# Fixed tensors for the probability buffers, and another sharing of the values products among a pair's five units

## The chip, the cores and the metric

The kernel runs on one core of one Trainium2 chip. The metric is the device time of one execution in microseconds (us), lower is better. Before the change three runs took 487.65, 487.83 and 488.74 us, so the median is 487.83 us.

## The reference

What is computed is an attention with a learned position bias, followed by a gated feed-forward stage with a convolution of three taps along the sequence. There are 4 batches, 8 heads, 576 positions and 64 columns per head; the feed-forward stage goes from 512 to 1024 and back to 512 columns.

```python
scores = scale * np.matmul(q, k.transpose(0, 1, 3, 2))
x = (psi_rel / psi_i)[..., None]
bias = np.maximum(x @ w1 + b1, 0.0) @ w2
scores = scores + bias.transpose(2, 0, 1)[None]
attn = np.exp(scores - scores.max(-1, keepdims=True))
attn = attn / (attn.sum(-1, keepdims=True) + 1e-09)
x = (attn @ v).transpose(0, 2, 1, 3).reshape(B, S, H * D)
h = np.maximum(x @ w_in, 0.0)
conv_out[i] = conv_w[0] * h[i - 1] + conv_w[1] * h[i] + conv_w[2] * h[i + 1]
out = (h / (1 + np.exp(-conv_out))) @ w_out
```

## The kernel before, in words

The program has three stages. In the first, some 65 us long, the bias table is computed on PE, DVE and ACT and stored to DRAM, and the first units of attention are slipped in. The second is attention, up to about 290 us. The third is the feed-forward stage, up to the end.

**Pairs and units.** Attention runs over 16 *pairs*: two heads of one batch (`seq`, index `n` from 0 to 15). The 576 query rows of a pair are cut into five *units* `t`: unit 0 holds the first 64 rows of both heads, units 1 to 4 hold 128 rows of each of the two heads. `flat` lists the units in order, pair after pair from `n = 1` on, with two units of pair 0 slipped in near the start; the list has 77 entries and `u` counts them. The main loop `for u, (n, t) in enumerate(flat)` works on three units at a time:

- `scores` (L364): products of the queries and keys of unit `u + 2` on PE, for one head after the other, each into one of the two PSUM buffers `s` (pool `psS`);
- `reduce` (L375): DVE adds the bias, scales, writes the result into a buffer `sp` in SBUF and keeps the row minimum in `nm`, for each head;
- `expo` (L389): ACT takes the exponential of unit `u + 1` in place in `sp`;
- `turned_sp` (L341 to L344): gives the buffer its second name `sr`, of the type that PE transposes (float32r). `sp` and `sr` are tiles of one pool under one tag, and ACT writes 128x2 elements of the new tile, behind the row (L343, the *tiny write*);
- `side_transposes` and `transposes` (L423, L435): PE turns the probabilities of unit `u`, 18 small products for a unit of two heads and 10 for unit 0. The last two of the 18 go into the free end of the PSUM buffer `s` of the scores just made (`side`); the other 16 go into two of three PSUM buffers `tp` (pool `psT`). Unit 2 of a pair also turns the row sums of the pair before (L427);
- copies (L92 on ACT, L95 on DVE): ACT copies the first `tp` buffer, DVE the `side` end and then the second `tp` buffer, into `ptx` (units 0 to 2) or `pty` (units 3 and 4);
- `part` (L472, from `pv_parts`): a *part* is two products of the turned probabilities with the values; five parts make the output of `ptx` (320 columns) and five that of `pty` (256 columns). The five of `ptx` are put into the queue `fill` when unit 2 is turned, those of `pty` when unit 4 is. The last part is followed by ACT's copy of the output from PSUM (L92, `x<-o`).

PE takes up to `pv_share[ui]` parts from `fill` after the transposes of unit `ui`. Before, the table is (2, 2, 1, 3, 2): units 3 and 4 do the five parts of `ptx`, units 0, 1 and 2 of the next pair those of `pty`. From `u = 7` (unit 0 of pair 2) on this table sets the order; before that the parts are taken as they come, and `u = 5` and `u = 6` (units 3 and 4 of pair 1) have none behind their transposes. Every product of scores and values stands as two records in the profile, every transpose as one.

Beside this, every second unit carries a job (`split_w_steps`) that prepares weights for the feed-forward stage: a shift on DVE (L101), a step on ACT (L103), a second shift on DVE in the next unit (L107), and two operations on GpSimd. The jobs start in every other unit; since a pair has five units, they fall on units 1 and 3 of the pairs with odd `n` (3 to 13) and on units 0, 2 and 4 of those with even `n`.

The order on each engine is the order of the program text. What holds an operation back is a buffer: the second head's scores need the `s` buffer that held the last unit's second head, so they wait for DVE's `reduce` and for DVE's copy of the `side` end; the second transpose of a unit needs the `tp` buffer that ACT copied in the unit before.

In the feed-forward stage `gt` and `hr` hold the last 64 rows of each batch; before, they are tiles of the pools `wo` and `hr`.

The lines that the change touches are L311 (the pool `sp`), L324, L330 to L344 (`new_sp`, `turned_sp`), L681 (`pv_share`), L783 (`gt`) and L859 (`hr`).

Of the kernel before, what the change touches and what calls it, by code (L numbers as in the profile page):

```python
# [9 lines left out]
F32 = mybir.dt.float32  # L10
F32R = mybir.dt.float32r
I32 = mybir.dt.int32
AF = mybir.ActivationFunctionType
# [6 lines left out]
def attention_ffn_kernel(  # L20
# [11 lines left out]
    nc = tc.nc  # L32
    B, S, DM = out.shape
# [5 lines left out]
    P = 128  # L39
    TL = S % P  # L40
# [4 lines left out]
    FC = DFF // P  # L45
# [13 lines left out]
    def pool(stack, name, bufs, **kw):  # L59
        return stack.enter_context(tc.tile_pool(name=name, bufs=bufs, reuse_waits="tile", **kw))  # L60

    const = pool(ctx, "const", 1)
    bias_c = const
    dram = ctx.enter_context(tc.tile_pool(name="dram", bufs=1, space=DRAM))
# [50 lines left out]
    def narrow(tp, raw, tags=("u", "w")):  # L115
        w, u = narrow_tiles(tp, raw, tags)
        for _ in narrow_steps(w, u, raw):
            pass
        return w.bitcast(F32)
# [19 lines left out]
    with tc.manual_schedule():  # L139
        att = ExitStack()  # L140
# [64 lines left out]
        pars = bias_c.tile([P, par.shape[1]], F32, name="pars")  # L205
# [102 lines left out]
            nc.sync.dma_start(dst[:, :, 0:nr + nf], st[:, :, 0:nr + nf])  # L308


        sp_p = pool(att, "sp", 1)  # L311
        ptx_p = pool(att, "ptx", 1)
        pty_p = pool(att, "pty", 1)
        sm_p = pool(att, "sm", 4)
# [6 lines left out]

        xb = {0: x0}
        spt, ptt, nms, exps = {}, {}, {}, {}
        SPB = 3  # L324
        DATA = mybir.DependencyInfo(mybir.DependencyClass.Sync, mybir.DependencyReason.DATA)

        def new_sp(n, t):  # L330
            tag = f"sp{len(nms) % SPB}"
            tile = sp_p.tile([P, 2 * S + 2], F32, name="sp", tag=tag)
            if t:
                spt[n, t] = (tile[:, 0:2 * S].rearrange("p (h j) -> p h j", h=2), tag)
            else:
                if n == 0:
                    nc.vector.memset(tile[:, 0:TL], 0.0)
                    nc.vector.memset(tile[:, TL + S:P + S], 0.0)
                spt[n, t] = (tile[:, TL:TL + S].rearrange("p (h j) -> p h j", h=1), tag)

        def turned_sp(n, t):  # L341
            tile = sp_p.tile([P, 2 * S + 2], F32R, name="sr", tag=spt[n, t][1])
            nc.scalar.activation(tile[:, 2 * S:], pars[:, 0:2], AF.Copy)  # L343
            spt[n, t] = (tile, None)  # L344


        def scores(n, t, h):
# [194 lines left out]
        xr, hr = [], []  # L542
# [129 lines left out]
        for h in heads(flat[0][1]):  # L672
            expo(*flat[0], h)
        turned_sp(*flat[0])
        while fill:
            fill.popleft()()
# [1 line left out]
        psT = pool(ctx, "psT", 3, space=PSUM)  # L678
        psO = pool(ctx, "psO", 1, space=PSUM)
        psum.update(s=psS, tp=psT, o=psO)  # L680
        pv_share = (2, 2, 1, 3, 2)  # L681
        hs_ff = {}
        raw_w = {}
        job_steps = iter(())
# [3 lines left out]
        for u, (n, t) in enumerate(flat):  # L688
            p, b = seq[n]
# [14 lines left out]
            if u + 1 < NU:  # L704
                for h in heads(flat[u + 1][1]):
                    expo(*flat[u + 1], h)
                turned_sp(*flat[u + 1])
# [11 lines left out]
            if u + 2 >= NU:  # L719
                f = u + 2 - NU  # L720
# [55 lines left out]
        wo_p = pool(ff, "wo", 1)  # L776
        g_p[0] = pool(ff, "g", FC + 4)
        e2_p = pool(ff, "e2", 2)
        hr_p = pool(ff, "hr", 1)
        o_p = pool(ff, "oo", 3)  # L780

        wo += [wo_p.tile([P, 2, DM], F32R, name=f"wo{f}") for f in range(FE, FC)]
        gt = [wo_p.tile([P, 2, P], F32R, name=f"gt{f}") for f in range(FC)]  # L783

        def tap(b, f, h):
            cv = (e2_p if f % 4 > 1 else e_p).tile([P, S], F32, name="cv")
# [69 lines left out]
                    if 0 <= j - k < FC:  # L856
                        stage(b * FC + j - k, k)

        hr += [hr_p.tile([P, B - 1, TL], F32, name=f"hr{f}") for f in range(FC)]  # L859
        ws = [narrow(tp, raw_o[0][:, k], ("cv", "cv")) for k, tp in enumerate((e_p, e2_p))]  # L860
        xr.append(xa_p.tile([P, KC, 2, B, TL], F32R, name="xr", tag="x"))
        x_rest(0)
# [7 lines left out]
        for b in range(B):  # L870
# [25 lines left out]
            for c in range(KC):  # L896
# [5 lines left out]
                lambda f, gi, t=t: gs[b, f][:, gi, t * P:(t + 1) * P] for t in range(NT)  # L902
# [98 lines left out]
```

## Time and profile before

| what | value |
|---|---|
| median of three runs | 487.83 us |
| profiled execution, first to last instruction | 485.4 us |
| granted TensorE clock in the profiled execution | 1.000 |
| PE busy, weight loads (PEld) busy | 469.5 us (97%), 332.0 us (68%) |
| DVE busy | 361.1 us (74%) |
| ACT busy | 316.6 us (65%) |
| GpSimd (POOL) busy | 147.2 us (30%) |
| share of PE in the chain of work that ended last | 85% |

The profiled execution is known by its span alone, 485.4 us; it lies 2.4 us below the median of the runs, which is the time around the first and the last instruction. Busy times are those of the engines between these two instructions. A PE that the profile shows as busy may still have gaps, since the ends of products are modelled; the weight loads (PEld) show more plainly when PE's queue moved on, and their starts are used below as the clock of PE's queue. One row of a timeline has the start, the time it covers, the engine, the line, the operation, what is written and read with shapes, the number of records, and in brackets the idle time before it and what released it.

### The profile page before, as it was taken

The page shows a single profiled execution, that of the slowest core. Times are in us where ns is not written, and L with a number is a line of the kernel's source. Part 1 is how long each engine was busy: PE and PEld are TensorE (multiplying, and loading weights), DVE is VectorE, ACT ScalarE, POOL GpSimd, SP SyncE. Part 2 cuts the span into 40 slices and gives each one's busy share as a digit, 9 for nine tenths or more (in the row PEclk, how much of TensorE's full clock was granted, in tenths as well). Part 3 has the DMA queues.
Part 4 walks back from the last instruction along what each step waited for, and adds up shares of the span by engine and source line. Part 5 has one row for each costly group of instructions (what it writes and reads, how often), then busy time and mean ns, then how long its engine had stood idle before and what let it go on. Part 6 is the DMA issues. An engine that isn't in the chain of part 4 may idle for free.

```text
span 485.4 us, 10556 instructions
## 1 busy us (share of the span) xinstructions
PE 469.5 (97%) x3914; PEld 332.0 (68%) x3914; DVE 361.1 (74%) x873; ACT 316.6 (65%) x791; POOL 147.2 (30%) x221
## 2 busy tenths in 40 slices
PE   5978899999999999999999999999999999999996
PEld 2333366666666666666666668988888888888886
DVE  6999976788898889988897821694489238936971
ACT  6999886798888889888888832772254125424530
POOL 1000001355445726556446728006000600060000
PEclk9999999999999999999999999999999999999999
DMA  1799957587667896599761300000100200020003
GB/s 50 226 352 306 329 161 171 134 267 216 170 171 205 229 246 150 161 231 260 217 144 50 113 26 25 1 2 17 69 1 0 81 28 1 1 86 1 0 3 107
DMA packets 32582, 60.79 MB, mean 125 GB/s; under 512 B 7196, under 2 KB 15796, under 8 KB 32532
## 3 DMA queue, kind: packets, MB, share of 16 engines
q1 hardware_dynamic: 27380, 47.02, 33.4%
q0 software_dynamic: 4768, 12.77, 8.9%
q8 instruction: 31, 0.51, 0.5%
q10 hardware_dynamic: 384, 0.35, 0.2%
q14 instruction: 19, 0.16, 0.1%
HBM read 44.12 MB, written 15.98 MB: 124 GB/s over the span
## 4 chain that ended last, share of the span: by engine, by line
PE 85%; DVE 0%; issue 0%; DVEq 0%
PE s L548 20%; PE o L472 18%; PE s L364 16%; PE tp L820 16%; PE tp L435 9%; PE o L820 4%; PE s L423 1%; PE s L427 0%; DVE pty L95 0%; DVE sp L375 0%; DVE o L828 0%; PE tp L492 0%; DVE ptx L95 0%; PE tp L593 0%; DVEq L828 0%
## 5 line engine op out<-in xcount | busy, mean ns | idle before, releaser
L375 DVE CUSTOM_DVE_ANT_0 sp<-s,bt 128x576 f32<-128x576 f32 x144 | 103.9, 753 | 30.1 <-PE s L364 11.9
L389 ACT ACTIVATE sp<-sp,nm 128x576 f32<-128x576 f32 x144 | 109.9, 767 | 0.0
L364 PE MATMUL s<-qk 64*128 64x288 f32 (+1 forms) x640 | 93.0, 431 | 3.3 <-DVE nm L375 2.4
L548 PE MATMUL s<-xs,wi 128*128 128x512 f32 x384 | 88.6, 390 | 0.0
L548 PEld LDWEIGHTS s<-xs,wi 128*128 128x128 f32 x384 | 71.8, 188 | 15.8 <-issue 0.5
L364 PEld LDWEIGHTS s<-qk 64*128 64x128 f32 (+1 forms) x640 | 46.8, 175 | 44.7 <-DVE nm L375 15.5
L820 PE MATMUL tp<-wo,g 128*128 128x512 f32 x288 | 70.3, 389 | 0.0
L435 PE MATMUL tp<-identr,sr 64*128 64x64 f32 x1184 | 64.4, 247 | 1.3 <-ACT sp L389 1.3
L795 DVE SCALAR_TENSOR_TENSOR cv<-h,cw,cv 128x575 f32<-128x575 f32 x64 | 52.3, 818 | 16.8 <-ACT cv L790 14.8
L820 PEld LDWEIGHTS tp<-wo,g 128*128 128x128 f32 x288 | 54.0, 188 | 11.2
L435 PEld LDWEIGHTS tp<-identr,sr 64*128 64x128 f32 x1184 | 55.6, 136 | 7.5 <-ACT sp L389 1.9
L561 ACT ACTIVATE h<-s 128x512 f32<-128x512 f32 x32 | 19.1, 598 | 57.0 <-PE s L548 57.0
L252 DVE TENSOR_SCALAR y<-tl,inv,nb 128x576 f32<-128x576 f32 (+33 forms) x112 | 47.6, 503 | 0.1
L472 PE MATMUL o<-ptx,vt 128*64 128x320 f32 x300 | 46.8, 442 | 0.0
L472 PE MATMUL o<-pty,vt 128*64 128x256 f32 x320 | 44.2, 393 | 0.0
L269 PE MATMUL s<-y,pars 128*32 128x512 f32 (+8 forms) x352 | 42.1, 493 | 2.0 <-DVE y L252 1.0
L135 POOL TENSOR_SCALAR xs<-x 128x512 fp32r<-128x512 f32 (+1 forms) x16 | 11.3, 704 | 105.4 <-DVE gt L815 105.4
L499 POOL DMA_DIRECT2D r_d<-rt x16 | 10.0, 627 | 86.9 <-DVE rt L95 86.9
L801 ACT ACTIVATE cv<-cv 128x576 f32<-128x576 f32 x32 | 21.9, 683 | 21.9 <-DVE cv L795 21.8
L802 DVE SCALAR_TENSOR_TENSOR cv<-cv,h 128x576 f32<-128x576 f32 x32 | 24.1, 753 | 14.1 <-ACT cv L801 14.1
L269 PEld LDWEIGHTS s<-y,pars 128*32 128x32 f32 x352 | 14.9, 111 | 26.5 <-DVE y L252 12.0
L95 DVE COPY ptx<-tp 128x256 f32<-128x256 f32 (+1 forms) x64 | 32.0, 499 | 0.6 <-PE tp L435 0.4
(91 smaller groups left out, 661.3 us busy)
## 6 DMA issues: line engine op xcount, KB each, us to landing
qk<-in_qk_dram SPq DMA_DIRECT2D x32, 320.0 KB, 5.0
bias_d<-st SPq DMA_DIRECT2D x13, 607.0 KB, 5.6
bt<-bias_d POOLq DMA_DIRECT2D x24, 288.0 KB, 5.4
qk<-in_qk_dram SPq DMA_DIRECT2D x32, 144.0 KB, 5.4
rb<-r_d POOLq DMA_DIRECT2D x32, 144.0 KB, 3.0
vt<-in_v_dram SPq DMA_DIRECT2D x16, 256.0 KB, 5.7
raw_w<-in_moe_w_in_dram SPq DMA_DIRECT2D x16, 256.0 KB, 4.9
out_dram<-o SPq DMA_DIRECT2D x16, 256.0 KB, 2.0
```

Of the source, the lines that this page charges most:

```text
L95: nc.vector.tensor_copy(o, i)
L252: nc.vector.tensor_scalar(y, dist[:, 0:n], inv[:, ig:ig + 1], nb1, op0=ALU.mult, op1=ALU.max)
L269: nc.tensor.matmul(ps[32 * j:32 * j + 32, a // 512 if n > 512 else blk % 2, 0:min(n - a, 512)], w2b, ys[j][:, a:min(n, a + 512)], start=Tr ...
L364: nc.tensor.matmul(ps[po, a, 0:HS], qt[rows, qo:qo + po.stop - po.start], qt[rows, KO + hh * HS:KO + hh * HS + HS], start=True, stop=True,)
L375: nc.vector.tensor_tensor_reduce(out=halves(spt[n, t][0][:, h]), in0=ps[:, :, 0:HS], in1=halves(bt[:, h]), op0=ALU.add, op1=ALU.min, scale ...
L389: exps[n, t, h] = nc.scalar.activation(sp[:, h], sp[:, h], AF.Exp, bias=nm[:, h:h + 1], scale=-1.0, accum_out=sms[n][:, col:col + 1],)
L435: tr = nc.tensor.transpose(ps[a][:, TL * s:TL * s + TL].bitcast(F32R), spf[ra, j:j + P], identr[ra, ra])
L472: nc.tensor.matmul(po[D * h:D * h + D, 0:width], vt[:, slot, :], pt[:, blk, :], start=(c == 0), stop=(c == 4),)
L548: nc.tensor.matmul(ps, wi[c][:, pw, f * P:f * P + P], rhs(c, px), start=(i == 0), stop=(i == 3 * KC - 1))
L795: nc.vector.scalar_tensor_tensor(out=cv[:, o:o + S - 1], in0=h[:, i:i + S - 1], scalar=cw[:, f, kk:kk + 1], in1=cv[:, o:o + S - 1], op0=AL ...
L802: nc.vector.scalar_tensor_tensor(out=cv, in0=cv, scalar=1.0, in1=h, op0=ALU.add, op1=ALU.mult)
L820: nc.tensor.matmul(ps, lhs(f, gi), wo[f][:, wj, cs], start=(f == 0 and i == 0), stop=(f == FC - 1 and i == 2),)
```

## The change

The three probability buffers become fixed tensors at set addresses: one block `shared` of three times 1160 words per partition, and over it for each buffer a float32 name (`sps[0]`) and a float32r name (`sps[1]`). `turned_sp` hands out the second name and issues nothing; the 80 tiny writes of ACT (one per unit, 16 pairs of five) are gone, and three memsets of 128x8 on DVE clear the ends of the buffers once at the start. The tensors `gt` and seven of the eight `hr` of the feed-forward stage are put at fixed places in the same block. The table `pv_share` becomes (3, 2, 0, 5, 0): unit 3 does all five parts of `ptx`, and units 0 and 1 of the next pair do those of `pty`; units 2 and 4 have no part behind their transposes.

```diff
--- before.py
+++ after.py
@@ -59,6 +59,15 @@
     def pool(stack, name, bufs, **kw):
         return stack.enter_context(tc.tile_pool(name=name, bufs=bufs, reuse_waits="tile", **kw))
 
+    SPB = 3
+    SPW = 2 * S + 8
+    arena = nc.alloc_sbuf_tensor("shared", [P, SPB * SPW], F32)
+    base = nc.lookup_mloc(arena).addr
+
+    def shared_at(name, shape, dtype, words):
+        return nc.alloc_sbuf_tensor_at(name, shape, dtype, offset=base + 4 * words)[:]
+
+    sps = [[shared_at(f"s{x}{i}", [P, SPW], dt, i * SPW) for i in range(SPB)] for x, dt in (("p", F32), ("r", F32R))]
     const = pool(ctx, "const", 1)
     bias_c = const
     dram = ctx.enter_context(tc.tile_pool(name="dram", bufs=1, space=DRAM))
@@ -308,7 +317,6 @@
             nc.sync.dma_start(dst[:, :, 0:nr + nf], st[:, :, 0:nr + nf])
 
 
-        sp_p = pool(att, "sp", 1)
         ptx_p = pool(att, "ptx", 1)
         pty_p = pool(att, "pty", 1)
         sm_p = pool(att, "sm", 4)
@@ -321,15 +329,16 @@
 
         xb = {0: x0}
         spt, ptt, nms, exps = {}, {}, {}, {}
-        SPB = 3
+        for sr in sps[1]:
+            nc.vector.memset(sr[:, 2 * S:].bitcast(F32), 0.0)
         DATA = mybir.DependencyInfo(mybir.DependencyClass.Sync, mybir.DependencyReason.DATA)
 
 
 
 
         def new_sp(n, t):
-            tag = f"sp{len(nms) % SPB}"
-            tile = sp_p.tile([P, 2 * S + 2], F32, name="sp", tag=tag)
+            tag = len(nms) % SPB
+            tile = sps[0][tag]
             if t:
                 spt[n, t] = (tile[:, 0:2 * S].rearrange("p (h j) -> p h j", h=2), tag)
             else:
@@ -339,9 +348,7 @@
                 spt[n, t] = (tile[:, TL:TL + S].rearrange("p (h j) -> p h j", h=1), tag)
 
         def turned_sp(n, t):
-            tile = sp_p.tile([P, 2 * S + 2], F32R, name="sr", tag=spt[n, t][1])
-            nc.scalar.activation(tile[:, 2 * S:], pars[:, 0:2], AF.Copy)
-            spt[n, t] = (tile, None)
+            spt[n, t] = (sps[1][spt[n, t][1]], None)
 
 
         def scores(n, t, h):
@@ -678,7 +685,7 @@
         psT = pool(ctx, "psT", 3, space=PSUM)
         psO = pool(ctx, "psO", 1, space=PSUM)
         psum.update(s=psS, tp=psT, o=psO)
-        pv_share = (2, 2, 1, 3, 2)
+        pv_share = (3, 2, 0, 5, 0)
         hs_ff = {}
         raw_w = {}
         job_steps = iter(())
@@ -780,7 +787,7 @@
         o_p = pool(ff, "oo", 3)
 
         wo += [wo_p.tile([P, 2, DM], F32R, name=f"wo{f}") for f in range(FE, FC)]
-        gt = [wo_p.tile([P, 2, P], F32R, name=f"gt{f}") for f in range(FC)]
+        gt = [shared_at(f"gt{f}", [P, 2, P], F32R, f * 2 * P) for f in range(FC)]
 
         def tap(b, f, h):
             cv = (e2_p if f % 4 > 1 else e_p).tile([P, S], F32, name="cv")
@@ -856,7 +863,8 @@
                     if 0 <= j - k < FC:
                         stage(b * FC + j - k, k)
 
-        hr += [hr_p.tile([P, B - 1, TL], F32, name=f"hr{f}") for f in range(FC)]
+        hr += [shared_at(f"hr{f}", [P, B - 1, TL], F32, 2 * P * FC + f * (B - 1) * TL) for f in range(FC - 1)]
+        hr.append(hr_p.tile([P, B - 1, TL], F32, name="hr"))
         ws = [narrow(tp, raw_o[0][:, k], ("cv", "cv")) for k, tp in enumerate((e_p, e2_p))]
         xr.append(xa_p.tile([P, KC, 2, B, TL], F32R, name="xr", tag="x"))
         x_rest(0)
```

**PE, units 2 and 3 of a pair.** In the rows the names before the arrow are written, those after it read; `s` are the score buffers, `tp` the transposes, `o` the output, `vt` the values. Line numbers move by 7 (L364 becomes L371, L435 becomes L442, L472 becomes L479). Before, from unit 2's transposes:

```order
L435 MATMUL tp<-identr,sr 128x64 x16
L472 MATMUL o<-pty,vt_112 64x256 x2
L364 MATMUL s<-qk 64x288 x4
L423 MATMUL s<-identr,sr 128x64 x2
L435 MATMUL tp<-identr,sr 128x64 x16
L472 MATMUL o<-ptx,vt_113 64x320 x6
```

And now:

```order
L442 MATMUL tp<-identr,sr_58 128x64 x16
L371 MATMUL s<-qk 64x288 x4
L430 MATMUL s<-identr,sr_59 128x64 x2
L442 MATMUL tp<-identr,sr_59 128x64 x16
L479 MATMUL o<-ptx,vt_118 64x320 x10
```

The products of unit 2 (one part) have gone to unit 0, and unit 3 has ten products (five parts) in place of six.

**PE, unit 4 and unit 0 of the next pair.** Before, from unit 4's scores of the unit two ahead:

```order
L364 MATMUL s<-qk 128x288 x4
L423 MATMUL s<-identr,sr 128x64 x2
L435 MATMUL tp<-identr,sr 128x64 x16
L472 MATMUL o<-ptx,vt_113 64x320 x4
L364 MATMUL s<-qk 128x288 x4
L435 MATMUL tp<-identr,sr 128x64 x10
```

And now:

```order
L371 MATMUL s<-qk 128x288 x4
L430 MATMUL s<-identr,sr_60 128x64 x2
L442 MATMUL tp<-identr,sr_60 128x64 x16
L371 MATMUL s<-qk 128x288 x4
L442 MATMUL tp<-identr,sr_58 128x64 x10
L479 MATMUL o<-pty,vt_118 64x256 x6
```

The two parts of unit 4 have gone to unit 3; unit 0's scores follow unit 4's transposes at once.

**ACT, units 1 and 2 of a pair with odd `n`.** Before, from the exponentials of unit 1's iteration to the copies of unit 2's (L103 is the step of a weight job, `x` the output of the attention, L92 all copies):

```order
L389 ACTIVATE sp,sm<-sp,nm 128x576 x2
L343 ACTIVATE sr<-pars 128x2
L92 ACTIVATE ptx<-tp 128x8x64
L103 ACTIVATE wu<-raw_w 128x256
L389 ACTIVATE sp,sm<-sp,nm 128x576 x2
L343 ACTIVATE sr<-pars 128x2
L92 ACTIVATE ptx<-tp 128x8x64
L92 ACTIVATE x_127<-o 128x256
```

And now (L396, L101 and L112 for L389, L92 and L103):

```order
L396 ACTIVATE sp_56,sm<-sp_56,nm 128x576 x2
L101 ACTIVATE ptx<-tp 128x8x64
L101 ACTIVATE x_133<-o 128x256
L112 ACTIVATE wu<-raw_w 128x256
L396 ACTIVATE sp_57,sm<-sp_57,nm 128x576 x2
L101 ACTIVATE ptx<-tp 128x8x64
```

The tiny writes are gone, and the copy of the output (`x<-o`) stands ahead of the second two exponentials, in place of behind the copy that follows them.

## Rows read from the trace of the kernel before

**Rows 1.** Busy time by engine over one pair, 180.26 to 194.49 us (first line: its columns).

```profile
core 0: us, PE busy (x) PEld busy (x) DVE busy (x) ACT busy (x) POOL busy (x), PEclk, DMA share, GB/s
180.26:194.49 14.23, 14.23 (x166) 9.43 (x164) 12.77 (x36) 12.19 (x35) 7.80 (x12) 1.00 0.66 164
```

**Rows 2.** Timeline, weight loads of units 2, 3, 4 and 0, 184 to 200 us.

```profile
188.74 0.79 PEld L364 LDWEIGHTS s<-qk 64*128 64x128 f32 x8 [0.38 <-DVE ptx L95]
...
189.88 0.73 PEld L435 LDWEIGHTS tp<-identr,sr 64*128 64x128 f32 x16
...
190.65 0.20 PEld L472 LDWEIGHTS o<-pty,vt 128*64 128x64 f32 x4
...
191.96 0.72 PEld L435 LDWEIGHTS tp<-identr,sr 64*128 64x128 f32 x16
...
192.73 1.27 PEld L472 LDWEIGHTS o<-ptx,vt 128*64 128x64 f32 x12
...
194.49 0.79 PEld L364 LDWEIGHTS s<-qk 64*128 64x128 f32 x8 [0.49 <-issue]
...
196.34 0.74 PEld L472 LDWEIGHTS o<-ptx,vt 128*64 128x64 f32 x8
...
197.57 0.79 PEld L364 LDWEIGHTS s<-qk 64*128 64x128 f32 x8 [0.49 <-DVE pty L95]
...
198.41 0.64 PEld L435 LDWEIGHTS tp<-identr,sr 64*128 64x128 f32 x10
```

**Rows 3.** Timeline, weight loads of units u = 6 and 7, 81 to 85 us.

```profile
81.58 0.78 PEld L364 LDWEIGHTS s<-qk 64*128 64x128 f32 x8
...
82.65 0.72 PEld L435 LDWEIGHTS tp<-identr,sr 64*128 64x128 f32 x16
83.32 0.30 PEld L364 LDWEIGHTS s<-qk 64*128 64x128 f32 x4
84.17 0.33 PEld L364 LDWEIGHTS s<-qk 64*128 64x128 f32 x4 [0.55 <-PE s L364]
84.52 0.67 PEld L435 LDWEIGHTS tp<-identr,sr 64*128 64x128 f32 x10
```

**Rows 4.** Timeline, weight loads of units u = 0 and 1, 64 to 68 us.

```profile
64.39 0.79 PEld L364 LDWEIGHTS s<-qk 64*128 64x128 f32 x8 [0.49 <-ACT sr L343]
...
67.41 0.67 PEld L435 LDWEIGHTS tp<-identr,sr 64*128 64x128 f32 x10
```

**Rows 5.** Timeline, DVE's copy of the side end, 83 to 85 us.

```profile
83.77 0.28 DVE L95 COPY pty<-s 128x128 f32<-128x128 f32 x1
```

**Rows 6.** Timeline of ACT, units 1 and 2 of an odd pair, 188 to 192 us.

```profile
188.51 0.43 ACT L103 ACTIVATE wu<-raw_w 128x256 f32<-128x256 f32 x1
188.83 0.77 ACT L389 ACTIVATE sp<-sp,nm 128x576 f32<-128x576 f32 x1
...
189.59 0.77 ACT L389 ACTIVATE sp<-sp,nm 128x576 f32<-128x576 f32 x1
...
190.48 0.20 ACT L343 ACTIVATE sr<-pars 128x2 fp32r<-128x2 f32 x1
190.76 0.60 ACT L92 ACTIVATE ptx<-tp 128x512 f32<-128x512 f32 x1
191.38 0.39 ACT L92 ACTIVATE x<-o 128x256 f32<-128x256 f32 x1
191.66 0.77 ACT L389 ACTIVATE sp<-sp,nm 128x576 f32<-128x576 f32 x1
```

**Rows 7.** Timeline, last pair, ACT's copy and PE's next transposes, 275 to 279 us.

```profile
275.42 0.74 PEld L435 LDWEIGHTS tp<-identr,sr 64*128 64x128 f32 x16
...
276.30 0.60 ACT L92 ACTIVATE ptx<-tp 128x512 f32<-128x512 f32 x1 [0.69 <-PE tp L435]
...
276.87 0.80 PEld L435 LDWEIGHTS tp<-identr,sr 64*128 64x128 f32 x16
```

**Rows 8.** Waits of the stretch 0 to 80 us: total, times, longest.

```profile
PEld s L423 <- ACT sp L389: 2.1, 2, 1.9
...
PEld tp L435 <- ACT sp L389: 1.9, 1, 1.9
```

**Rows 9.** Groups by line and form: the smallest memset on DVE.

```profile
L337 DVE MEMSET sp<- 128x64 f32 x1 | 0.1, 112 | 0.0
```

## Prediction

> **What bounds the kernel now.** I read the busy times by stretch first, then the timeline of PE's weight loads over one pair, then ACT and DVE where PE's steps end. Over one pair, 14.23 us long, PE is busy for all 14.23 us, DVE for 12.77 and ACT for 12.19 [rows 1]. The reader is to see that attention goes at PE's pace, so a shorter ACT queue alone gives nothing. The question is whether PE's own queue gets shorter, and whether something that PE used to meet in time is now late.
>
> For PE's queue I measure from start to start of weight loads. Twelve records of a 320-column product take 192.73 to 194.49, 1.76 us, and eight take 196.34 to 197.57, 1.23 us [rows 2]. The difference of four records is 0.53 us, so a record streams for 0.1325 us and 8 x 0.1325 = 1.06 us of the 1.23 us are streaming. The other 0.17 us are the price of going from products to the next scores. A 256-column record is taken as 0.8 of that, 0.106 us.
>
> **What the change moves, and the price of each part.** The products are the same ones, so their streaming (0.1325 or 0.106 us a record) only changes its place. Per pair two of five places where PE goes from transposes to products to scores become transposes to scores. With products, the transposes take 0.77 us (189.88 to 190.65) [rows 2], and 0.17 us go behind the products: 0.94 us without streaming. Where unit u = 6 has no products, the scores start 0.67 us after the transposes (82.65 to 83.32) [rows 3]. So 0.27 us of PE's queue are saved at each place, if nothing else holds PE. The Trainium skill's page "TensorEngine Tiling (Array Packing)", section "Key Properties", says that changing the tiling mode drains TensorE; products and scores are in different modes here, so by that rule alone the change would save at every place that it clears, which is the first rival below. The rows show that it does not end there.
>
> *Term A, unit 4 to unit 0 of the next pair.* Before, from unit 4's scores to unit 0's transposes: 194.49 to 198.41, 3.92 us, less 1.06 us of streaming, 2.86 us [rows 2]. Without products the trace has the same passage at u = 6 to 7: 81.58 to 84.52, 2.94 us [rows 3], and at u = 0 to 1: 64.39 to 67.41, 3.02 us [rows 4]. The saved 0.27 us are there, but the second head's scores start 0.85 us after the first head's (83.32 to 84.17), where unhindered both heads take 0.84 us (197.57 to 198.41) [rows 2, 3], so 0.42 for one. What they wait for is their PSUM buffer, whose side end DVE copies from 83.77 to 84.05 [rows 5]. So the 0.27 us are paid back with some more: 0.08 us at u = 6, 0.16 us at u = 0. I take 0.10 us, since the first of these is the nearer one (a unit 4, followed by a unit 0). There are 13 such passages (pair 2 to 3 up to pair 14 to 15): **+1.3 us**, between +1.0 (0.08) and +2.1 (0.16).
>
> *Term B, unit 2 to unit 3.* From unit 2's transposes, at T, to unit 3's: 189.88 to 191.96, 2.08 us, less 4 x 0.106 = 0.42 of streaming: 1.66 us [rows 2]. Unit 3's scores and side transposes take 2.08 - 0.77 - 0.42 - 0.17 = 0.72 us of this. Without products PE would be there at T + 0.67 + 0.72 = T + 1.39, or T + 1.56 if entering unit 0's smaller score products costs 0.17 too. But unit 3's second transpose needs the buffer that ACT empties in unit 2. ACT's copy starts at T + 0.88 (189.88 to 190.76) [rows 2, 6]. The last pair shows the bound: the copy starts at T + 0.88 and ends at T + 1.48 (276.90), and the transposes that start at T + 1.45 take 0.80 in place of 0.72 us [rows 7], so they can start no sooner than T + 1.53. With the copy on time, unit 3 gains 1.66 - 1.53 = 0.13 us.
>
> Is it on time? ACT's copy of the output now stands ahead of the exponentials. It starts 0.31 us after the streaming ends (190.65 + 0.42 to 191.38) and holds ACT for 0.28 us (to 191.66) [rows 2, 6]. Unit 1's streaming ends at 188.74 - 0.17 = 188.57 [rows 2], so the copy starts at 188.88 and ACT is free at 189.16. In odd pairs the job step follows, 0.32 us (188.51 to 188.83), then two exponentials of 0.76 us (188.83 to 189.59) [rows 6]: ACT is free for unit 2's copy at 189.16 + 0.32 + 1.52 = 191.00, 0.24 us later than T + 0.88 = 190.76. That turns the gain of 0.13 into a loss of 0.11 us. In even pairs there is no job step there: 190.68, in time. Here the missing tiny write helps: with it ACT would be free 0.33 us later (189.59 + 0.76 = 190.35 against 190.68, the tiny write's end) [rows 6]. Seven even pairs (2 to 14) and six odd (3 to 13): -7 x 0.13 + 6 x 0.11 = **-0.25 us**, between 13 x -0.13 = -1.7 and 13 x 0.11 = +1.4.
>
> *Term C, the end of attention.* In pair 15 no scores stand between unit 2's and unit 3's transposes. Both before and after they start at T + 1.53 at the earliest, but before, the 0.42 us of streaming fitted in that wait [rows 7]; now they come later: +0.42. Behind unit 4 the first feed-forward products follow at once: -0.27. **+0.15 us.**
>
> *Term D, the first 80 us.* Three memsets of 8 columns on DVE, ahead of the bias table; the smallest one there is, of 64 columns, takes 0.112 us [rows 9], so at most 0.34, taken as +0.2 us. PE waits for exponentials three times there, 2.1 + 1.9 us [rows 8]; a tiny write ahead of one delays it by 0.33 us at most, so between -1.0 and 0, taken as -0.2 us. **0 us.**
>
> The other tiny writes cost nothing and give nothing: ACT's spare 14.23 - 12.19 = 2.04 us a pair [rows 1] hide them, and their worth is in B already. Unit 3 with five parts is long (about 4.3 us), so DVE empties its queue there, its slack of 14.23 - 12.77 = 1.46 us [rows 1] is used up in one place, and it starts unit 4 without a backlog, as in the passage of A. The output is read by GpSimd two pairs later, so its earlier copy releases nobody. `gt` and `hr` are first written when the buffers below them have long been read, so I cost them at nothing; if not, the first feed-forward products would wait, under 1 us once.
>
> The sum: 1.3 - 0.25 + 0.15 + 0 = +1.2 us on the profiled span of 485.4 us. The median of the runs is 487.83 us, 2.4 us above that span, a part that the change leaves alone: **489.0 us**. A measurement of this kernel can tell about 0.2%, 1.0 us, from no change.
>
> **The rivals.** (1) *Every cleared switch is saved.* The drain alone counts and DVE and ACT keep up: 13 x 2 x -0.27 = -7.0 us, 480.8 us. Against it stand both passages without products in this trace, which waited [rows 3, 4]. (2) *ACT gets ahead, the other side of the forecast.* Without tiny writes ACT is early in all pairs, the output's copy does not hold the exponentials, and DVE starts unit 4's row minimum sooner, so A is 0.04 in place of 0.10: 13 x (-0.13 + 0.04) = -1.2, 486.8 us with C. It decides where ACT is free before T + 0.88 in odd pairs too, which wants 0.24 us more than I find. (3) *The copies come later still.* A is 0.16, and the copy of the output makes ACT 0.24 us late in even pairs as well, 0.35 in odd: 13 x 0.16 + 7 x 0.11 + 6 x 0.22 = 4.2, 492.1 us. For it speaks that DVE's second minimum now also waits for an event of ACT's. (4) *Nothing nets out*: A and B cancel and the fixed tensors only take ACT work that was hidden: 487.8 us.
>
> **How the numbers follow.** My forecast has 0.46, with its own range 488.0 to 490.3 (A and B at their middle bounds); rival 1 has 0.05, rival 2 0.20, rival 3 0.16, rival 4 0.13. The range of 8 in 10 leaves out rival 1 and the outer half of rivals 2 and 3: 486.2 to 491.3. Slower by over 1.0 us are two thirds of the forecast (0.30) and rival 3: 0.46. Faster by over 1.0 us are rival 1 and most of rival 2 (0.15): 0.20. The rest is 0.34.
>
> **What would show it.** Right: the period of a pair goes from 14.23 to about 14.2 in even and 14.4 us in odd pairs; in unit 0 the second head's scores start about 0.85 us after the first head's, released by DVE's side copy; unit 3's transposes start about 1.53 (even) or 1.77 us (odd) after unit 2's. Wrong: a period below 14.1 us, with the two heads' scores of unit 0 at 0.42 us distance, or above 14.6 us.

## The result, and the profile after

The change takes **490.88 us** (median of 6 runs, 489.63 to 491.25), the kernel before 487.57 us (6 runs, 487.13 to 488.74): a ratio of **1.0064, with a 95% interval of 1.0053 to 1.0075**. It is slower by 3.3 us. The forecast said slower too, 489.0 us with a range of 486.2 to 491.3: the time lies inside the range, but the rise is nearly three times the 1.2 us of its middle.

The page after, busy time by engine and the chain that ended last:

```profile
PE 469.9 (96%) x3914; PEld 335.5 (69%) x3914; DVE 359.4 (73%) x876; ACT 301.8 (62%) x711; POOL 147.6 (30%) x221
...
PE 80%; DVE 7%; DMA 6%; ACT 5%; issue 2%; SPq 0%; DVEq 0%; ACTq 0%
```

The span is 489.1 us against 485.4. Busy time in four pairs after (these answer to [rows 1]; the first two from unit 3's scores to unit 3's, the last two from unit 4's to unit 4's; us, PE, PEld, DVE, ACT, POOL, granted clock, DMA share, GB/s):

```profile
91.90:106.23 14.33, 14.13 (x167) 9.58 (x165) 10.90 (x33) 10.28 (x28) 6.70 (x13) 1.00 0.91 251
106.23:120.74 14.51, 14.33 (x166) 9.69 (x164) 12.22 (x37) 11.16 (x30) 7.78 (x13) 1.00 0.85 233
168.27:183.16 14.89, 14.20 (x166) 9.84 (x164) 12.12 (x36) 11.27 (x29) 5.64 (x9) 1.00 0.98 260
183.16:197.78 14.62, 14.54 (x166) 9.53 (x164) 13.70 (x36) 10.95 (x28) 8.43 (x12) 1.00 0.66 155
```

Before, every pair took 14.22 to 14.24 us from unit 3 to unit 3. Now the periods are by turns 14.2 to 14.3 and 14.5 us; the mean of the twelve from 91.90 us on is 14.45. Two pairs are disturbed: the last two lines, 14.89 and 14.62 us, where the others take 14.3 to 14.5 us from unit 4 to unit 4. PE is no longer busy all the time, though ACT has some 1 us less to do.

PE's weight loads after, from unit 2 of an even pair to unit 0, and (from 105.45) units 2 and 3 of the odd pair behind it. They answer to [rows 2, 3]:

```profile
91.12 0.73 PEld L442 LDWEIGHTS tp<-identr,sr 64*128 64x128 f32 x16
...
92.63 0.75 PEld L442 LDWEIGHTS tp<-identr,sr 64*128 64x128 f32 x16
93.42 2.35 PEld L479 LDWEIGHTS o<-ptx,vt 128*64 128x64 f32 x20
96.26 0.79 PEld L371 LDWEIGHTS s<-qk 64*128 64x128 f32 x8 [0.49 <-issue]
...
97.34 0.73 PEld L442 LDWEIGHTS tp<-identr,sr 64*128 64x128 f32 x16
98.02 0.30 PEld L371 LDWEIGHTS s<-qk 64*128 64x128 f32 x4
98.94 0.33 PEld L371 LDWEIGHTS s<-qk 64*128 64x128 f32 x4 [0.62 <-PE s L371]
99.29 0.66 PEld L442 LDWEIGHTS tp<-identr,sr 64*128 64x128 f32 x10
100.00 1.06 PEld L479 LDWEIGHTS o<-pty,vt 128*64 128x64 f32 x12
...
105.45 0.74 PEld L442 LDWEIGHTS tp<-identr,sr 64*128 64x128 f32 x16
...
106.96 0.95 PEld L442 LDWEIGHTS tp<-identr,sr 64*128 64x128 f32 x16
107.95 2.35 PEld L479 LDWEIGHTS o<-ptx,vt 128*64 128x64 f32 x20
```

The reader is to see two things. In unit 0 the first head's scores start 0.68 us after unit 4's transposes (97.34 to 98.02), the second head's only 0.92 us later (98.94), and the row names a wait. In unit 3 the sixteen transposes take 0.75 us in the even pair and 0.95 in the odd one. DVE in the same passage:

```profile
97.18 0.76 DVE L382 CUSTOM_DVE_ANT_0 sp<-s,bt 128x576 f32<-128x576 f32 x1 [2.38 <-PE s L371]
...
97.86 0.75 DVE L382 CUSTOM_DVE_ANT_0 sp<-s,bt 128x576 f32<-128x576 f32 x1
...
98.54 0.28 DVE L104 COPY pty<-s 128x128 f32<-128x128 f32 x1
```

The side copy ends at 98.82, and 0.12 us later the second head's scores start in the buffer that it has read, just as at u = 6 in [rows 3, 5]. Summed over the pairs from 94 to 270 us, the waits of the weight loads. After:

```profile
PEld s L371 <- PE s L371: 6.9, 12, 0.6
```

and before:

```profile
PEld s L364 <- DVE pty L95: 6.4, 13, 0.5
```

Of the 13 waits of about 0.5 us behind unit 4's products, none is left; in their place stand 12 of about 0.6 us in front of the second head's scores (the thirteenth lies behind 270 us). The old 0.5 us were no loss of that size: the loads stand idle as long behind unit 3's products, where nothing is named (0.49 at 96.26). (The row names PE's earlier scores, which had ended long before; experiment e7 shows which instruction the wait is for.)

### The profile page after: what moved, and what is told of

Read it like the earlier page. It is cut to its first block, busy times and chain, and to the rows that moved or that the text cites. A ratio compares the mean times of both kernels' runs of the same rounds, so it can differ in the third digit from the quotient of the medians.

```text
span 489.1 us, 10524 instructions
## 1 busy us (share of the span) xinstructions
PE 469.9 (96%) x3914; PEld 335.5 (69%) x3914; DVE 359.4 (73%) x876; ACT 301.8 (62%) x711; POOL 147.6 (30%) x221
## 4 chain that ended last, share of the span: by engine, by line
PE 80%; DVE 7%; DMA 6%; ACT 5%; issue 2%; SPq 0%; DVEq 0%; ACTq 0%
PE s L555 20%; PE tp L827 16%; PE o L479 15%; PE s L371 13%; PE tp L442 7%; PE o L827 4%; DVE sp L382 3%; DMA vt<-in_v_dram 3%; PE s L278 2%; DVE y L261 2%; DMA bias_d<-st 2%; ACT sp L396 1%; ACT st L304 1%; ACT y L257 1%; DVE ptx L104 1%
## 5 line engine op out<-in xcount | busy, mean ns | idle before, releaser
L396 ACT ACTIVATE sp<-sp,nm 128x576 f32<-128x576 f32 x144 | 110.0, 768 | 0.2
L371 PE MATMUL s<-qk 64*128 64x288 f32 (+1 forms) x640 | 96.8, 435 | 4.9 <-DVE nm L382 2.2
L371 PEld LDWEIGHTS s<-qk 64*128 64x128 f32 (+1 forms) x640 | 46.0, 174 | 40.2 <-issue 12.1
L442 PE MATMUL tp<-identr,sr 64*128 64x64 f32 x1184 | 66.3, 248 | 2.4 <-ACT sp L396 2.0
L442 PEld LDWEIGHTS tp<-identr,sr 64*128 64x128 f32 x1184 | 57.3, 136 | 8.5 <-ACT sp L396 2.6
L479 PE MATMUL o<-ptx,vt 128*64 128x320 f32 x300 | 43.7, 437 | 0.7 <-DMA vt<-in_v_dram 0.5
L479 PE MATMUL o<-pty,vt 128*64 128x256 f32 x320 | 41.2, 389 | 0.0
L101 ACT ACTIVATE x<-o 128x256 f32<-128x256 f32 (+1 forms) x31 | 12.7, 410 | 36.0 <-PE o L479 36.0
L101 ACT ACTIVATE ptx<-tp 128x256 f32<-128x256 f32 (+1 forms) x64 | 26.6, 442 | 13.0 <-PE tp L442 12.6
```

Of the source, the lines that this page charges most:

```text
L101: nc.scalar.activation(o, i, AF.Copy)
L371: nc.tensor.matmul(ps[po, a, 0:HS], qt[rows, qo:qo + po.stop - po.start], qt[rows, KO + hh * HS:KO + hh * HS + HS], start=True, stop=True,)
L396: exps[n, t, h] = nc.scalar.activation(sp[:, h], sp[:, h], AF.Exp, bias=nm[:, h:h + 1], scale=-1.0, accum_out=sms[n][:, col:col + 1],)
L442: tr = nc.tensor.transpose(ps[a][:, TL * s:TL * s + TL].bitcast(F32R), spf[ra, j:j + P], identr[ra, ra])
L479: nc.tensor.matmul(po[D * h:D * h + D, 0:width], vt[:, slot, :], pt[:, blk, :], start=(c == 0), stop=(c == 4),)
```

## The experiments

My theory was the forecast's: the loss is the wait for unit 4's buffer (A), and unit 2's gain is kept only where ACT's copy is in time (B). Against it stood that the fixed tensors cost or save time by themselves, or that the loss lies in unit 2. All runs were read by two passages of PE's queue, from start to start of weight loads, and compared **less the streaming of the products in them** (0.42 us for one part in unit 2, 1.06 for two in unit 4). *T2 to P3*: from unit 2's transposes to unit 3's products (term B). *S4 to P0*: from unit 4's scores to unit 0's products (term A). "To the end" is the span less the start of the first load of unit 3's scores (77.66 us before, 78.10 after), since the stretch ahead of it varies by over a microsecond from run to run whatever is edited.

| kernel | shares | median us | ratio, 95% interval | T2 to P3, even / odd | S4 to P0 | to the end |
|---|---|---|---|---|---|---|
| before | 2,2,1,3,2 | 487.6 | 1 | 2.43 / 2.43 | 3.54 | 407.7 |
| change | 3,2,0,5,0 | 490.88 | 1.0064, 1.0053 to 1.0075 | 2.30 / 2.51 | 3.63 or 3.73 | 411.0 |
| e1, e5 tensors only | 2,2,1,3,2 | 488.54, 488.93 | 1.0015, 0.9998 to 1.0031; 1.0034, 1.0021 to 1.0047 | 2.44 / 2.44 | 3.54 | 408.2 |
| e2 shares only | 3,2,0,5,0 | 492.12 | 1.0083, 1.0064 to 1.0102 | 2.42 / 2.74 | 3.63 or 3.73 | 412.2 |
| e3 unit 4 only | 2,2,1,5,0 | 490.26 | 1.0052, 1.0034 to 1.0071 | 2.43 / 2.43 | 3.63 or 3.73 | 410.2 |
| e4 unit 2 only | 3,2,0,3,2 | 487.90 | 1.0004, 0.9993 to 1.0016 | 2.30 / 2.50 | 3.54 | 408.2 |
| e6 unit 1 short | 4,1,0,3,2 | 488.19 | 1.0029, 1.0009 to 1.0049 | 2.30 / 2.50 | 3.54 | 408.4 |
| e7 side copy on ACT | 3,2,0,5,0 | 489.97 | 1.0056, 1.0043 to 1.0069 | 2.30 / 2.51 | 3.64 or 3.75 | 410.3 |
| e8 both | 4,1,0,5,0 | 490.41 | 1.0063, 1.0051 to 1.0075 | 2.30 / 2.51 | 3.64 or 3.75 | 410.5 |
| e9 step moved | 3,2,0,3,2 | 487.07 | 0.9994, 0.9985 to 1.0002 | 2.30 / 2.30 | 3.54 | 406.6 |
| e10 change, step moved | 3,2,0,5,0 | 489.20 | 1.0031, 1.0019 to 1.0043 | 2.29 / 2.29 | 3.63, twice 3.74 | 409.0 |

The kernel before took 487.78 us beside e1 to e4, 487.40 beside e5 to e8 and 487.68 beside e9 and e10.

### e1 and e5: the fixed tensors without the shares

```diff
-        pv_share = (3, 2, 0, 5, 0)
+        pv_share = (2, 2, 1, 3, 2)
```

> The fixed tensors alone, with the table of before (2, 2, 1, 3, 2). Theory (the new sharing makes the loss, the fixed tensors only cost something in the first 80 us): the period of a pair is 14.23 us as before, from unit 4's scores to unit 0's products 4.60 us, from unit 2's transposes to unit 3's products 2.85 us; the time is that of before plus up to 0.4 us, 487.6 to 488.0 us. Rival (the second row minimum's new wait for ACT, or the fixed places themselves, cost in every unit): period 14.3 us or more, 489.5 us or more.

> The change without its table of shares: fixed tensors for the probability buffers, the old shares 2, 2, 1, 3, 2. Both theories: time within 0.3% of before (487.6 us), span near 485.5 us; from unit 2's transposes to unit 3's products 2.85 us and from unit 4's scores to unit 0's products 4.60 us in every pair, as before. The theory that nothing of the loss lies in the fixed tensors asks for periods of 14.23 us and for no cost of the three memsets at the head; the rival, that the missing tiny write makes ACT run ahead and frees time by itself, asks for a period under 14.15 us.

The profiled execution of e1 took 1516.51 us, three times as long as its other runs, so the passages are read from e5, the same kernel again. They are those of before to 0.01 us, and the period is 14.24 us: in the pairs the tiny writes alone had cost PE nothing, and their absence alone frees nothing. The three memsets take DVE from 4.58 us on for 0.10 us in the change, and the next instruction starts 0.32 us after the one ahead of them, as it did before. Both medians lie above before all the same. Of e5's profiled execution, 1.70 us of its 2.2 us more lie in the first 78 us (79.36 against 77.66), and there the clock had fallen. e5, stretches of 2 us:

```profile
48.00:50.00 2.00, 0.42 (x8) 0.00 (x0) 1.48 (x3) 1.43 (x3) 0.00 (x0) 1.00 0.92 349
50.00:52.00 2.00, 1.82 (x8) 0.50 (x12) 2.00 (x7) 2.00 (x4) 0.00 (x0) 0.62 1.05 413
52.00:54.00 2.00, 2.00 (x16) 0.57 (x10) 2.00 (x6) 0.21 (x1) 0.00 (x0) 0.53 1.04 409
```

before, the same place:

```profile
48.00:50.00 2.00, 0.47 (x6) 0.24 (x4) 1.69 (x5) 1.63 (x3) 0.00 (x0) 1.00 1.05 415
50.00:52.00 2.00, 2.00 (x19) 0.69 (x18) 2.00 (x5) 2.00 (x4) 0.00 (x0) 1.00 1.04 408
```

In both PE stands idle there, 1.75 us in e5 and 1.53 before; behind it the granted clock fell to 0.62 and 0.53 in e5, so near 1.2 GHz in place of 2.4, and stayed at 1.00 before. What is missing to full clock is 2 x 0.38 + 2 x 0.47 = 1.7 us, as much as e5 is late at 79.36. e4, e6 and e9 have the same fixed tensors, kept the full clock at this place, and pass unit 3's scores at 77.42, 77.42 and 78.42 us, so the trace gives no sign that the tensors make the head late.

The tensors are not free, though. At a mean granted clock of 0.998 or more, five runs of e1 and e5 (without that of 1516.51 us) have a median of 488.06 us and the twenty of the kernel before beside them 487.19. Of these 0.9 us, 0.5 are the time that e5 needs longer to the end (408.2 against 407.7): half of them lie at one place in the last pair, read with term C below, the rest is 0.01 us a pair and 0.1 us behind the last pair's unit 3. Where the others lie stays open; five runs are few.

### e2: the shares without the fixed tensors

```diff
-        pv_share = (2, 2, 1, 3, 2)
+        pv_share = (3, 2, 0, 5, 0)
```

(in the kernel before)

> The new sharing alone, on the pool tiles with the tiny writes. Theory (ACT's queue sets unit 3's transposes, and the missing tiny write gives it 0.24 to 0.33 us back): from unit 2's transposes to unit 3's products about 2.5 us in even and 2.8 us in odd pairs, where the changed kernel has 2.30 and 2.51; unit 4's scores to unit 0's products as in the changed kernel, 3.63 to 3.73; the time is about 493 us, 2 to 3 us more than the changed kernel. Rival (ACT has the time, tiny writes never matter): the same places as in the changed kernel, 490.5 us.

Slowest of all, and at the place named: the tiny write makes ACT late by another 0.12 us in even pairs (2.42 against 2.30) and 0.23 in odd ones (2.74 against 2.51). Unit 2 and 3 of an odd pair in e2, weight loads:

```profile
104.64 0.73 PEld L435 LDWEIGHTS tp<-identr,sr 64*128 64x128 f32 x16
...
106.61 0.72 PEld L435 LDWEIGHTS tp<-identr,sr 64*128 64x128 f32 x15 [0.33 <-ACT ptx L92]
107.37 1.54 PEld L472 LDWEIGHTS o<-ptx,vt 128*64 128x64 f32 x14
```

(The view ends at 109 us, within the last row's products.)

So the two halves of the change belong together: 7 x 0.12 + 6 x 0.23 = 2.2 us of the shares' loss are avoided by the fixed tensors, which save nothing by themselves. To the end e2 is only 1.2 us behind the change (412.2 against 411.0), since the change pays the tensors' 0.5 us and has the two disturbed pairs.

### e3 and e4: one cleared unit each

```diff
-        pv_share = (3, 2, 0, 5, 0)
+        pv_share = (2, 2, 1, 5, 0)
```

> Fixed tensors, unit 4 alone without products, table (2, 2, 1, 5, 0). Theory (this place carries the loss: 0.10 to 0.20 us in each of 13 pairs): unit 4's scores to unit 0's products 3.63 to 3.73 us, less streaming 0.09 to 0.20 us more than before; unit 2's transposes to unit 3's products 2.85 as before; time 489.5 to 490.3 us. Rival (both places lose alike, or only the combination of both loses): 488.5 to 489.0 us.

```diff
-        pv_share = (3, 2, 0, 5, 0)
+        pv_share = (3, 2, 0, 3, 2)
```

> Fixed tensors, unit 2 alone without products, table (3, 2, 0, 3, 2). Theory (this place gives 0.13 us in even pairs and loses 0.09 us in odd pairs; 0.4 to 0.8 us are lost once in the last pair): unit 2's transposes to unit 3's products 2.30 and 2.51 us, time 487.8 to 488.8 us. Rival (this place carries the loss): 489.5 us or more.

Clearing unit 4 costs what the change costs there (S4 to P0 is 3.63 or 3.73 in both); to the end it adds 410.2 - 408.2 = 2.0 us. Clearing unit 2 adds 0.0 to the end. The change itself is at 411.0; the 0.8 us that neither run has are the two disturbed pairs. A weight-load row of e3, unit 0's second head, is the change's row again:

```profile
98.53 0.33 PEld L371 LDWEIGHTS s<-qk 64*128 64x128 f32 x4 [0.63 <-PE s L371]
```

### e6: does the output copy hold the odd pairs?

```diff
-        pv_share = (3, 2, 0, 5, 0)
+        pv_share = (4, 1, 0, 3, 2)
```

> The change with shares 4, 1, 0, 3, 2: unit 4 keeps its two parts (so no loss there), unit 2 has none, and unit 1 has one part in the place of two, so that the output copy leaves ACT about 0.42 us sooner in the odd pairs. Theory (unit 3 is held in odd pairs by ACT, which copies the transposed probabilities late because the output copy stands ahead of it): from unit 2's transposes to unit 3's products 2.30 us in even and odd pairs alike, against 2.30 and 2.51 with shares 3, 2, 0, 3, 2; 13 x (2.43 - 2.30) = 1.7 us less than before, 485.9 us. Rival 1: the output copy isn't what holds ACT, odd pairs stay at 2.5, 487.9 us as with 3, 2, 0, 3, 2. Rival 2: unit 1, now shorter, makes unit 2's second scores wait for the copy from their buffer, as in unit 4: the same 0.15 us a pair as there, and 13 x 0.15 = 2.0 us are lost again, 487.9 us, with the wait in front of the second head's scores in unit 2.

Rival 1: the odd pairs stay at 2.50. The output copy did come earlier (ACT took it straight behind its other copy), but the conversion's step stands behind it. ACT in an odd pair of e6:

```profile
103.55 0.38 ACT L101 ACTIVATE x<-o 128x256 f32<-128x256 f32 x1
103.83 0.43 ACT L112 ACTIVATE wu<-raw_w 128x256 f32<-128x256 f32 x1
104.15 0.76 ACT L396 ACTIVATE sp<-sp,nm 128x576 f32<-128x576 f32 x1
```

That left the step itself as the suspect, and led to e9.

### e7 and e8: the side copy of unit 4 on ACT

```diff
-                dve(halves(d0[:, 8, c0:c0 + P]), side[:, :, HS:HS + TL])
+                (act if t == 4 else dve)(halves(d0[:, 8, c0:c0 + P]), side[:, :, HS:HS + TL])
```

(e8: the same, with shares 4, 1, 0, 5, 0)

> The change whole, with one line more: in unit 4 the copy of the 128 columns out of the scores buffer (0.28 us) goes from DVE to ACT, which is idle then. Theory (unit 0's second scores wait for that copy, which stands on DVE behind both row minima): the buffer comes free at the end of the second row minimum, about 0.25 us sooner; from unit 4's scores to unit 0's products 3.45 us in the place of 3.63 to 3.73; 13 x 0.24 = 3.1 us less than the change, 487.8 us. Rival 1: another wait sets the place (the copies of the transposed values, the first row minimum's late start): 3.63 to 3.73 as before, 490.9 us. Rival 2: the copy delays ACT's own copy of the transposed probabilities there and the exponentials behind it: later than 3.73, over 491 us.

> The change with shares 4, 1, 0, 5, 0 and unit 4's copy out of the scores buffer on ACT: both cures together. Theory: from unit 2's transposes to unit 3's products 2.30 us in all pairs, from unit 4's scores to unit 0's products 3.45 us; against the change 13 x 0.24 + 6 x 0.21 = 4.4 us less, 486.5 us, about 1 us below the kernel before. Rival: one of the two cures opens a new wait (unit 2's second scores, or ACT), and it stays at or above 487.8 us.

The wait moved with the copy and didn't shrink. e7, the second head's scores in unit 0, then ACT, then DVE:

```profile
99.28 0.30 PEld L371 LDWEIGHTS s<-qk 64*128 64x128 f32 x4 [0.67 <-ACT pty L101]
...
98.95 0.28 ACT L101 ACTIVATE pty<-s 128x128 f32<-128x128 f32 x1 [1.06 <-DVE nm L382]
...
98.15 0.75 DVE L382 CUSTOM_DVE_ANT_0 sp<-s,bt 128x576 f32<-128x576 f32 x1
```

The first line settles what the scores wait for: the side copy, whichever engine makes it. The second shows why the cure fails: ACT had been free for 1.06 us, but the program orders its read of the buffer behind DVE's second row minimum, which reads the same buffer, so the copy starts when the minimum ends and not beside it. My theory named the right copy, and wrongly took its place on DVE for the reason that it is late; both kernels came out at rival 1, the first in e7's list, and not at the theory's 487.8 and 486.5 us. e8 adds that unit 1 with one part is harmless but useless, as in e6.

### e9 and e10: the conversion's step a unit later

```diff
-            next(job_steps, None)
+            for _ in range(0 if t == 1 and u % 2 else 2 if t == 2 and u % 2 == 0 else 1):
+                next(job_steps, None)
             del spt[n, t]
```

(e9 with shares 3, 2, 0, 3, 2; e10 with the change's)

> The change with shares 3, 2, 0, 3, 2 and one line more: the steps of the weight conversion that stood behind unit 1's products are taken a unit later in the odd pairs, so that ACT's step (0.43 us) no longer stands between the output copy and unit 2's exponentials. Theory (odd pairs hold unit 3's transposes because that step makes ACT late with its copy of unit 2's transposed probabilities): from unit 2's transposes to unit 3's products 2.30 us in all pairs, in the place of 2.30 and 2.50; 6 x 0.20 = 1.2 us less than shares 3, 2, 0, 3, 2 alone, 486.7 us, nearly 1 us below the kernel before. Rival: ACT is late in odd pairs for another reason and they stay at 2.50, 487.9 us. Second rival: the step in its new place delays unit 3's exponentials and with them unit 4's transposes, and the gain is lost there.

> The change whole with the same line: conversion steps of odd pairs a unit later. Theory: from unit 2's transposes to unit 3's products 2.30 us in all pairs, but from unit 4's scores to unit 0's products still 3.63 to 3.73; 1.2 us less than the change, 489.7 us, still 2 us above the kernel before, because the wait for unit 4's buffer stays. Rival: the moved step also changes when DVE gets to unit 4's row minima (its own conversion steps move as well), and the 3.63 and 3.73 change by 0.1 or more.

The theory held: 2.28 to 2.30 in all thirteen pairs of e9. Its odd pair, PE's weight loads, then ACT:

```profile
105.55 0.73 PEld L442 LDWEIGHTS tp<-identr,sr 64*128 64x128 f32 x16
...
107.05 0.75 PEld L442 LDWEIGHTS tp<-identr,sr 64*128 64x128 f32 x16
107.84 1.27 PEld L479 LDWEIGHTS o<-ptx,vt 128*64 128x64 f32 x12
...
106.42 0.60 ACT L101 ACTIVATE ptx<-tp 128x512 f32<-128x512 f32 x1
106.92 0.43 ACT L112 ACTIVATE wu<-raw_w 128x256 f32<-128x256 f32 x1
```

The transposes take 0.75 us in place of 0.95, and the step stands behind the copy that PE waits for. To the end e9 needs 406.6 us, 1.1 less than before: 13 x 0.13 = 1.7 us of term B, less 0.5 us from unit 3's scores in the last pair to the end (223.5 us against 223.0), most of it the 0.42 us of streaming that term C had forecast to be lost there. Its median of 487.07 us is the lowest of all, but by 0.9994, with an interval up to 1.0002, it is not told apart from before. In e10 the same line takes 2.0 us off the change to the end and as expected leaves it slower than before: 1.3 us at unit 3 (6 x 0.22), and, as its rival had it, 0.6 us from unit 4's wait, where six of the eight long passages have become short ones (6 x 0.10). One pair of e10 is disturbed too (14.91 us from unit 3 to unit 3).

## Why the prediction was right, and what was mis-sized

The direction was right, and so were the mechanisms of A and B. That the time stayed inside the range is in part luck: the span grew by 3.7 us where the sum had 1.2, A, C and what no term held all missed upwards, and the range was wide because rival 3 had been allowed for.

**Rival 1, every switch saved, fell.** The saving itself is there: 0.68 us from unit 4's transposes to the next scores, where products in between need 0.94 us without streaming. The rule of the Trainium skill's page "TensorEngine Tiling (Array Packing)", section "Key Properties", that a change of mode drains TensorE, agrees with that. But by the table, unit 4's 0.27 us a pair are paid back with 0.16 on top, and unit 2's are kept by half at best. Rival 3 had 0.16 for A, which is what came, but its reason was the second row minimum, and here it is the first that starts late; the loss in even pairs that it added isn't there.

**Term A was the right mechanism, under-sized: +1.3 forecast, +2.0 measured.** The step that failed is "I take 0.10 us, since the first of these is the nearer one". There are two cases, and the nearer passage was no guide to their number: 8 of 13 passages take 3.73, 5 take 3.63, a mean of 3.69 against 3.54, 0.156 a pair and 13 x 0.156 = 2.0 us. Of this, 0.13 a pair lie in the forecast's own passage, up to unit 0's transposes (3.01 to 3.03 us, as 96.26 to 99.29, or 2.92, against 2.85): the long case is that of u = 0, which I had set aside (3.02). The other 0.03, from unit 0's transposes to its products (0.71 us against 0.68), the forecast had not counted. The upper bound given was +2.1. The short case in the change, weight loads, then DVE:

```profile
125.09 0.79 PEld L371 LDWEIGHTS s<-qk 64*128 64x128 f32 x8 [0.49 <-issue]
...
127.65 0.33 PEld L371 LDWEIGHTS s<-qk 64*128 64x128 f32 x4 [0.52 <-PE s L371]
...
125.89 0.76 DVE L382 CUSTOM_DVE_ANT_0 sp<-s,bt 128x576 f32<-128x576 f32 x1 [1.49 <-PE s L371]
```

Here the first row minimum starts 0.80 us after the scores' first load (125.09 to 125.89), in the long case 0.92 (96.26 to 97.18), and the second head's scores follow 2.56 and 2.68 us after unit 4's. At u = 6, the passage that I had chosen, it was 0.84 (81.58 to 82.42), because DVE was still at work until then, which I had not looked at: that is neither of the two cases.

**Term B was right in both halves.** -0.13 in even pairs is 2.30 against 2.43; +0.11 in odd pairs came out as +0.08. The job step as the reason is shown by e9, the missing tiny write as help by e2. One sign came otherwise: unit 3's transposes start 1.51 us after unit 2's in odd pairs too (105.45 to 106.96), and not 1.77; the wait for ACT lies within the sixteen. What I had not in the sum is one even pair at 2.84, below.

**Term C, +0.15, was nearer +0.6.** From unit 2's scores in the last pair to the end it is 211.28 us against 211.12, and after has 0.42 us less streaming left there. Unit 3's transposes do start at T + 1.53 (278.96 to 280.49), as said; the step that failed is that the products then follow freely. The change, weight loads of the last pair, then DVE:

```profile
280.49 0.72 PEld L442 LDWEIGHTS tp<-identr,sr 64*128 64x128 f32 x15 [0.55 <-ACT ptx L101]
281.49 2.35 PEld L479 LDWEIGHTS o<-ptx,vt 128*64 128x64 f32 x20 [0.28 <-DVE ptx L104]
...
279.68 0.76 DVE L382 CUSTOM_DVE_ANT_0 sp<-s,bt 128x576 f32<-128x576 f32 x1 [0.18 <-ACT sp L396]
```

They wait another 0.28 us for DVE's copy, since DVE's second row minimum starts late. This isn't the new sharing. e2 has the shares of the change and no such wait; e5 has those of before and waits. e2, then e5:

```profile
281.11 0.72 PEld L435 LDWEIGHTS tp<-identr,sr 64*128 64x128 f32 x15 [0.55 <-ACT ptx L92]
281.87 2.35 PEld L472 LDWEIGHTS o<-ptx,vt 128*64 128x64 f32 x20
...
278.74 0.81 PEld L442 LDWEIGHTS tp<-identr,sr 64*128 64x128 f32 x16
279.85 1.30 PEld L479 LDWEIGHTS o<-ptx,vt 128*64 128x64 f32 x12 [0.30 <-issue]
```

From unit 2's transposes in the last pair to unit 3's products it is 2.53 to 2.55 us in the change and in e3 to e6, and 2.29 or 2.30 before, in e2 and in e7 to e10. So 0.25 of the 0.6 us come with the fixed tensors, for which the sum had nothing at this place, and go again with other small edits; e2, without the tensors, loses some 0.25 us in the last pair where the sum had 0.15. Why DVE's minimum starts late stays open: in the change the row names ACT, in e5 no wait ends there.

**Term D, nothing, was right as far as it can be told**: three memsets cost 0.1 us of DVE and delay nothing. The 0.44 us by which the change's profile is late at 78 us are within what that stretch varies (77.42 to 79.36 us in the runs with fixed tensors).

**Two pairs were in no term.** In the pair at 14.89 us the products of unit 3 waited for the values' load, which landed at 180.19 us (the row names a shift on DVE that had ended at 179.74); chain of waits and weight loads of the change:

```profile
166.65 13.54 DMA vt<-in_v_dram
...
180.29 2.38 PEld L479 LDWEIGHTS o<-ptx,vt 128*64 128x64 f32 x20 [0.58 <-DVE wu L110]
```

That load took 13.54 us where the median is 6.8; its data are now wanted 0.55 us earlier, so the change has less room for such a load, though one instance does not show how often it matters. In the next pair DVE was late:

```profile
186.13 1.22 DVE L110 TENSOR_SCALAR wu<-raw_w 128x256 int32<-128x256 int32 x1
...
185.77 1.42 POOL L519 TENSOR_TENSOR x<-x,rb 128x576 f32<-128x576 f32 x1 [4.95 <-ACT pty L101]
```

The same DVE instruction takes 0.27 to 0.29 us in most places; here it ended 0.16 us after GpSimd's (187.35 and 187.19). The Trainium skill's page "SBUF — State Buffer", section "SBUF: two separate sides", says that the two engines share one pair of ports, which some of their instructions take under a lock that the loser waits out whole; the rows agree. The change has three more such instances, of 1.50 us, at 138.10, 196.63 and 253.87, each ahead of an idle stretch of DVE; the kernel before has them too, one of 1.53 us at 193.82.

The sum of the change's 3.7 us of span, rounded terms: A 2.0, five-part unit 3 0.3 (2.845 us where 1.765 + 1.06 were due, 13 times), C 0.6, B 0.0 with the late load in it, the second disturbed pair and unit 0's products 0.4 (what is left, not measured one by one), the head 0.4.

## What to carry to other kernels

Work that fills PE between two steps may also be the time in which a buffer comes free: before it is moved away, find the place where the trace already runs without it, and read every such place as a case of its own, with the start of each instruction in it, rather than choose between two numbers. Of the two cleared places here, the one whose next step needs one scores buffer gained where ACT was in time, and the one whose next step needs both lost. Where every other period is longer, look for a step with another cadence than the loop (here a conversion every two units in a loop of five) and move that step, not the loop's own work.

## What the runs showed of the hardware

**A row minimum that waits for PE and for ACT starts 0.1 us later than one that waits for PE alone.** In the change's trace, those that found DVE idle and whose instruction has a wait for PE alone start 0.80 or 0.81 us after the first load of their scores; with a wait for ACT added it is 0.90 to 0.92, without exception among the 26 from 85 to 275 us. That is what makes the two cases of term A: the first row minimum of unit 4 starts at 0.90 to 0.92 in the eight long passages and at 0.80 or 0.81 in the five short ones. In e10, where the steps fall otherwise, it has no wait for ACT in eleven of the thirteen, and these are the short ones. The trace shows the wait for PE as an instruction by itself there, 97.07 to 97.09 in the long case, 0.81 us after the first load, where otherwise the row minimum starts; that one follows at 97.18 with its wait for ACT, whose last event lay 0.32 us back. So the 0.1 us goes with the second instruction, not with what ACT does; an experiment on it was not made.

**The granted clock behind an idle stretch of PE does not go by its length alone**: at the same place of the program it was 0.62 and 0.53 behind 1.75 us of waiting in e5, but 1.00 behind 1.53 us in the kernel before and 1.00 behind 2.11 us in e9. Of the 58 runs of the kernel before that stand beside the experiments, the 30 with a mean granted clock of 0.998 or more have a median of 487.26 us, the 24 with 0.995 or 0.996 one of 487.79.
